# A stream of Fourier, mixing and token steps on one core: product sums over two steps, other buffers, later weight tasks

## The chip, the cores and the metric

One core of a Trainium2 chip runs the whole program. The metric is the device time of one execution in microseconds. Times of one kernel vary by some tenths of a per cent between runs, so a median of runs is given. The profile is of one further execution.

## What is computed

```
X = rfft(x, axis=1)                         # x: 8 x 3008 x 256
Yr = Xr @ w_r - Xi @ w_i + b_r ; Yi = Xr @ w_i + Xi @ w_r + b_i
Y = soft_threshold(Yr, 0.01) + 1j * soft_threshold(Yi, 0.01)
a = irfft(Y, n=3008, axis=1)                # 8 x 3008 x 256
u = a + (relu(a^T @ w_tok1) @ w_tok2)^T     # w_tok1: 3008 x 256, w_tok2: 256 x 3008
out = u + relu(u @ w_ch1) @ w_ch2           # w_ch1: 256 x 1536, w_ch2: 1536 x 256
```

The weights of the last two lines come as 64-bit numbers and are narrowed to 32 bits on the chip. Products that need full precision are made of three, with each operand split into a high and a low part (`hi * hi + hi * lo + lo * hi`).

## The kernel before

The length 3008 is 47 x 64, and the transform is done in two stages. The batch is worked in five *units*: batch entries 0 and 1 alone, then three pairs (`UNITS`, line 23). Three parts of the program follow each other.

**The start** (`begin`) takes unit 0 through the transform, makes the transformed token weights, and runs the 47-point stage of unit 1 beside it, one *row* at a time. A unit has 13 rows (`NG`). `row47` does one row n and prepares the following: it loads the row n + 4 (SP queue), makes the sum and the difference of the two halves of row n + 2 (`sum_diff`, lines 253 to 259: sum on GpSimd, L257, difference on VectorE, L258, into a tile `sd`), splits row n + 1 into high and low parts (ScalarE casts, VectorE subtracts into `xl`), and multiplies row n (`stage1`, products named `p`, six of 512 columns for a unit of two entries), evicts it on ScalarE and stores it to `a_d`. From its iteration 7 on (`FIRST47`) the start does a row in each of its remaining 15 iterations. The mixing weights are kept as sums in tiles of the tags `gh` and `gl` until `split_mix` splits them.

**The stream** (`stream`) takes units 1 to 4 through the 64-point stage, the mixing and the way back, in 84 steps: 12 for unit 1 and 24 for each pair, a step being one pair of frequencies and one batch entry. An iteration n works on several steps at once:

```
mix_a(n - 2)    6 products into p1 (bank "pm"); VectorE adds the bias: p2 = p1 + bias (L561)
forward2(n)     4 products px; ScalarE and VectorE split the result into xth and xtl, GpSimd a third of xtl (L550)
inverse(n - 4)  6 products pi for each pair of steps, evicted by ScalarE and stored to b_d
tokens(n - 4 or n - 5)  12 products gp, accumulated over the unit
mix_b(n - 2)    12 products added to p2 (named p); soft threshold z on ScalarE and VectorE; yh on ScalarE, yl on GpSimd
row47()         at some n: a row of the next unit (at47 spreads the 13 rows over the steps of the unit before)
tasks           loads, widenings and stores of the channel and token weights, 90 pieces at an even pace
```

`MIX` is the 2 and `LAG` the 4. The two p2 banks are used in turn; `p1`, `px`, `pi`, `pm` and the row's `p` share four PSUM banks that go round (`bank`, tag `w`). A widening (`narrow`, L167 to L177) is two ScalarE and six VectorE operations. `PACE` spreads the 90 pieces from n = 2 on, 1.25 x 90 / 84 = 1.34 in each n. The order in each engine's queue is laid out by a scheduler when the program is built.

**The channel stage** (`channel7`) takes the 24064 tokens in 24 chunks of 1024 (the last 512). In a chunk, 42 slots t each issue three products of the first channel product (`sx`, `sw`, `fq`) and three of the second (`s`), in an order written out by hand and kept. Between them stand the token products for the next chunk: a *group* of 4 or 5 times 94 tokens has two parts (`make_parts`), each six products with the weights `wt` and eight or ten small ones with `b`, into one bank `pu` that ScalarE then copies to `uf`. A chunk has two or three groups, and a table `makes` says at which slot each part stands: the last group at 22 and 26, the one before at 13 and 17, the first of three at 4 and 8. When the second part is issued, the loads of the next group are issued on SP (`load_wt2`, `load_b2`). Where that group is the first of a unit, `fetch_g` loads `gh` and `gl` of the unit after it first (L421).

Of the kernel before, what the change touches and what calls it, by code (L numbers as in the profile page):

```python
# [11 lines left out]
F32 = mybir.dt.float32  # L12
# [29 lines left out]
AT = (0, 3, 4, 1, 5, 6, 2)  # L42
MIX, LAG = 2, 4
FIRST47 = 7
PACE = 1.25

# [85 lines left out]
def tile_kernel(ctx: ExitStack, tc: tile.TileContext, io):  # L132
# [9 lines left out]
    dram = ctx.enter_context(tc.tile_pool(name="dram", bufs=1, space=bass.MemoryType.DRAM))  # L142
    ps = ctx.enter_context(tc.tile_pool(name="ps", bufs=4, space=bass.MemoryType.PSUM))
    sums, pairs2 = ExitStack(), ExitStack()
# [82 lines left out]
    def ev(shape, name):  # L227
        return wk.tile(shape, F32, tag="ev", name=name, bufs=2)

    def t4(shape, name):  # L230
        return wk.tile(shape, F32, tag="t4", name=name, bufs=2)
# [20 lines left out]

    def sum_diff(x, g, w, eng, pool):
        if eng is None:
            return x
        sd = wk.tile([120, 2, w], F32, tag="xf", name="sd", bufs=2) if pool is None else wk.tile([120, 2, w], F32, tag=("xtl", "xf", "et")[g % 3], name="sd", bufs=3 if g % 3 == 0 else 2)
        eng.tensor_tensor(out=sd[:, 0], in0=x[:, 0], in1=x[:, 1], op=ALU.add)  # L257
        V.tensor_tensor(out=sd[:, 1], in0=x[:, 0], in1=x[:, 1], op=ALU.subtract)  # L258
        return sd
# [6 lines left out]
    def stage1(sd, dst, g, w, pool):  # L266
        n = GS if g < NG - 1 else N2 - GS * (NG - 1)
        a = ev([120, 2, w], "a") if pool is None else pool.tile([120, 2, w], F32, name="a", bufs=3)
        each = 512 // w
        for i0 in range(0, 2, each):  # L270
            pt = bank("p1")
            for i in range(i0, i0 + each):
                o = (i - i0) * w
                if pool is None:
                    mm3(pt[:, o:o + w], f1r[:, 0, i], f1r[:, 1, i], sd[0][:, i], sd[1][:, i], True, True)
                else:
                    PE.matmul(pt[:120, o:o + w], lhsT=f1[:, i], rhs=sd[:, 0], start=True, stop=False)
                    PE.matmul(pt[:120, o:o + w], lhsT=f1[:, 2 * i], rhs=sd[:, 1], start=False, stop=True)
            S.copy(out=a[:, i0:i0 + each].rearrange("p i w -> p (i w)"), in_=pt[:120])
        rows = dst.rearrange("(i n) k w -> (n k) i w", i=2)  # L280
        PUT.dma_start(out=rows[g * 120:g * 120 + n * KH, :, :w], in_=a[:n * KH])
# [142 lines left out]
    def parts(u):  # L424
# [40 lines left out]
        def forward(kp, b, a2):  # L465
            pt = bank("px")
            for t in range(2):
                for ab in range(2):
                    o = (2 * t + ab) * 128
                    PE.matmul(pt[:, o:o + 128], lhsT=a2[:, ab, b, t * 128:(t + 1) * 128], rhs=f2cols(2 * kp + ab), start=True, stop=True)  # L470
            xf = wk.tile([128, 3, 4, 64], F32, tag="xth", name="xf", bufs=3)
            S.copy(out=xf[:, 1:3], in_=pt.rearrange("p (q i m) -> p i q m", i=2, m=64))
            V.tensor_tensor(out=xf[:, 0], in0=xf[:, 1], in1=xf[:, 2], op=ALU.add)
            return xf
# [20 lines left out]
        def inverse(kp, e, y, pool=None):  # L495
            bt = ev([128, 2, w], "bt") if pool is None else pool.tile([128, 2, w], F32, name="bt", bufs=3)
            each = 512 // w
            for i0 in range(0, 2, each):
                pt = bank("pi")
                for i in range(i0, i0 + each):  # L500
                    o = (i - i0) * w
                    if plain:
                        PE.matmul(pt[:, o:o + w], lhsT=e[:, i], rhs=y[:, i], start=True, stop=True)
                    else:
                        mm3(pt[:, o:o + w], e[:, 0, i], e[:, 1, i], rows(y, 0, i), rows(y, 1, i), True, True)
                S.copy(out=bt[:, i0:i0 + each].rearrange("p i w -> p (i w)"), in_=pt)
            PUT.dma_start(out=bdv[kp, :, :, :, :w], in_=bt)
# [27 lines left out]
        def forward2(b, a2, kp):  # L535
            pt = bank("px")
            for t in range(2):
                for ab in range(2):
                    o = (2 * t + ab) * 128
                    PE.matmul(pt[:, o:o + 128], lhsT=a2[:, ab, b, t * 128:(t + 1) * 128], rhs=f2cols(2 * kp + ab), start=True, stop=True)  # L540
            xh = wk.tile([128, 3, 4, 64], F32R, name="xth", bufs=3)
            xl = wk.tile([128, 3, 4, 64], F32R, name="xtl", bufs=3)
            xs = wk.tile([128, 4, 64], F32, name="xs", bufs=2)
# [14 lines left out]
        def mix_a(xt, p2):  # L558
            p1 = bank("pm")[:, :C]
            part(p1, xt, 0, 0, True)  # L560
            V.tensor_tensor(out=p2.rearrange("p (i c) -> p i c", i=2), in0=p1.rearrange("p (o c) -> p o c", o=1).to_broadcast([128, 2, C]), in1=bias, op=ALU.add)  # L561
# [20 lines left out]
    def beside(u):  # L582
# [7 lines left out]
        def add(g):  # L590
            if g < NG:
                sums_[g] = sum_diff(xs.pop(g), g, p.w, G, None)

# [26 lines left out]
    def stream(tasks):  # L620
# [3 lines left out]
        for i, (u, g) in enumerate(rows47):  # L624
            if u == 1 or i < done47["n"]:
                continue
            prev = first[u - 1]
            room = first[u] - 3 - prev
            at47.setdefault(prev + g * room // NG, []).append(i)
        a2s, xts, ys, ets = {}, {}, {}, {}  # L630
# [26 lines left out]
        need(1)  # L657
        pace, left, finished = PACE * len(tasks) / len(steps), 0.0, 0
        for n in range(len(steps) + LAG + 2):
# [19 lines left out]
            for m in (n - LAG, n - LAG - 1):  # L679
                if 0 <= m < len(steps):  # L680
                    u, kp, b = steps[m]
                    if b == len(UNITS[u]) - 1 and (n - m == LAG) == (b == 0):
                        parts_of(u).tokens(kp, wts_[kp], ys.pop((u, kp)))
                        if kp == KP - 1:
                            parts_of(u).close()
            ready(n - 2)
            if 0 <= c < len(steps):
                u, kp, b = steps[c]
# [5 lines left out]
            for _ in at47.get(n, ()):  # L694
                row47()
            if n > 1:
                left += pace
# [12 lines left out]
    def weights_tasks(kind, p):  # L710
# [11 lines left out]
        def widen():  # L722
            t = got["t"] = wc["task"].tile([128, 2, 512], F32, tag="wide", name="wide")
            narrow(got.pop("raw"), t[:, 0], t[:, 1])
# [29 lines left out]
    def tokens_tasks(i, jt):  # L754
# [9 lines left out]
        def widen():  # L764
            t = wc["task"].tile([128, 2, 512], F32, tag="wide", name="wide")
            wf = narrow(got.pop("raw")[:, :n], t[:, 0, :n], t[:, 1, :n])
            o = wc["task"].tile([128, 2, 512], F32R, tag="so", name="so")
            split(o[:, 0, :n], o[:, 1, :n], wf, S, V)
            got["o"] = o
# [8 lines left out]
    def begin():  # L778
# [7 lines left out]
        with tc.tile_pool(name="early", bufs=1) as early:  # L786
# [25 lines left out]
            for n in range(NW + KP):  # L812
# [26 lines left out]
                if n == FIRST47 - 1:  # L839
# [5 lines left out]
                    sides[u].divide(g)  # L845
                if n >= FIRST47:
                    row47()
# [237 lines left out]
    def channel7():  # L1085
# [14 lines left out]
        wc["pu"] = ps3.tile([128, 512], F32, name="pu")  # L1100
        wc["fq"] = bank("fq")
        for g in needs[0]:
# [25 lines left out]
        for n in range(len(chunks)):  # L1128
# [3 lines left out]
            for i, g in enumerate(mine):  # L1132
                m = make_parts(g, True)
                first = 22 - 9 * (len(mine) - 1 - i)
                makes[first], makes[first + 4] = (m, g), (m, g)
            for g in range(2):
# [91 lines left out]
```

## Time and profile before

| | us |
|---|---|
| median of 3 runs | 2361.85 (2357.34 to 2363.17) |
| profiled execution | 2356.0 |
| its span | 2354.2 |
| TensorE busy in the span | 2267.6 (96%) |
| VectorE busy | 2024.0 (86%) |
| ScalarE busy | 1667.2 (71%) |
| GpSimd busy | 279.6 (12%), all in the start and the stream |
| mean granted TensorE clock | 0.988 |

The start ends at about 156 us of the span, the stream at about 713 us; the rest is the channel stage. A product's busy time includes its way through the array, and the next one starts before it ends, so that a busy share of 96% is not 96% of the pace that is possible: the pace is read from the starts of products.

### The profile page before, as it was taken

The numbers are of one execution on the slowest core, as the hardware profiler recorded it, in microseconds if no ns is written. First come the engines' busy times: TensorE is split into PE (matmuls) and PEld (weight loads), VectorE is DVE, ScalarE is ACT, GpSimd is POOL, SyncE is SP. The second block draws the span as 40 slices with busy tenths as digits, with TensorE's granted clock in tenths as the row PEclk, the third lists the DMA queues.
The fourth block names the chain that finished last, engine by engine and source line by source line (L and its number), as shares of the span: only waits on it lengthen the run. The fifth ranks groups of instructions, "written<-read, shape, count | busy, mean of one in ns | idle before, by whom it ended". The sixth has DMA issues, their size and how long they took to land.

```text
span 2354.2 us, 34225 instructions
## 1 busy us (share of the span) xinstructions
PE 2267.6 (96%) x11844; PEld 1939.2 (82%) x11844; DVE 2024.0 (86%) x3307; ACT 1667.2 (71%) x3156; POOL 279.6 (12%) x236
## 2 busy tenths in 40 slices
PE   8997999989999999999999999999999999999999
PEld 7777878779897878888888887888888888888887
DVE  7757998998744889979999997989998998998999
ACT  6566666677655777767777776777777777777776
POOL 0135554444330000000000000000000000000000
PEclk9998999999999999999999999999999999999999
DMA  8789887776537444454444445444545445445435
GB/s 212 229 260 310 266 273 228 248 242 233 197 125 247 142 142 145 142 163 136 138 131 150 148 139 159 138 136 138 150 149 151 148 130 149 125 141 160 144 106 161
DMA packets 205610, 407.88 MB, mean 173 GB/s; under 512 B 17093, under 2 KB 108829, under 8 KB 205437
## 3 DMA queue, kind: packets, MB, share of 16 engines
q1 hardware_dynamic: 175369, 351.16, 49.6%
q10 hardware_dynamic: 30068, 54.53, 6.9%
q8 instruction: 94, 1.54, 0.3%
q14 instruction: 79, 0.65, 0.1%
HBM read 303.00 MB, written 102.63 MB: 172 GB/s over the span
## 4 chain that ended last, share of the span: by engine, by line
PE 73%; DVE 8%; DMA 5%; ACT 1%; issue 1%; POOL 0%; SPq 0%; POOLq 0%; ACTq 0%; DVEq 0%
PE s L945 27%; PE sx L945 16%; PE sw L945 8%; PE pu L945 5%; PE pu L911 5%; PE fq L945 4%; PE p L556 3%; DMA b<-b_d 2%; DMA wt<-wt_d 1%; PE px L540 1%; PE pm L556 1%; DVE sd L258 1%; PE gp L204 1%; PE gp L205 1%; DVE p L561 1%
## 5 line engine op out<-in xcount | busy, mean ns | idle before, releaser
L945 PE MATMUL s<-rh,a2s 128*128 128x512 f32 (+1 forms) x2016 | 775.4, 387 | 0.8 <-ACT rh L153 0.8
L945 PE MATMUL sx<-ub,a 128*128 128x512 f32 (+1 forms) x1728 | 489.4, 392 | 1.8 <-DVE c L1001 1.1
L945 PEld LDWEIGHTS s<-rh,a2s 128*128 128x128 f32 x2016 | 379.3, 189 | 77.1 <-ACT rh L153 1.4
L156 DVE TENSOR_TENSOR rl<-c,rh 128x512 fp32r<-128x512 f32 (+1 forms) x576 | 380.1, 677 | 57.7 <-ACT rh L153 49.3
L945 PE MATMUL s<-rl,a2s 128*128 128x512 f32 (+1 forms) x1008 | 390.6, 388 | 0.7 <-DVE rl L156 0.2
L153 ACT CAST rh<-c 128x512 fp32r<-128x512 f32 (+1 forms) x576 | 338.7, 612 | 57.7 <-DVE rl L1045 21.8
L945 PEld LDWEIGHTS sx<-ub,a 128*128 128x128 f32 x1728 | 319.1, 190 | 64.3 <-DVE c L1001 2.4
L945 PE MATMUL sw<-ub,a 128*128 128x512 f32 (+1 forms) x864 | 240.3, 387 | 1.4 <-DVE ub L156 1.1
L945 PEld LDWEIGHTS s<-rl,a2s 128*128 128x128 f32 x1008 | 190.0, 188 | 40.4 <-DVE rl L156 2.9
L153 ACT CAST rh<-r 128x512 fp32r<-128x512 f32 (+1 forms) x288 | 174.2, 613 | 50.0 <-PE s L945 37.4
L1070 DVE TENSOR_TENSOR uf<-s,uf 128x512 f32<-128x512 f32 (+1 forms) x288 | 194.3, 675 | 13.1 <-PE s L945 12.5
L156 DVE TENSOR_TENSOR rl<-r,rh 128x512 fp32r<-128x512 f32 (+1 forms) x288 | 189.3, 675 | 1.3
L945 PEld LDWEIGHTS sw<-ub,a 128*128 128x128 f32 x864 | 160.5, 188 | 35.0 <-DVE ub L156 1.4
L917 ACT COPY uf<-pu 128x470 f32<-128x470 f32 (+31 forms) x158 | 61.1, 415 | 147.5 <-PE pu L911 136.4
L911 PEld LDWEIGHTS pu<-g,b 96*128 96x128 f32 x1024 | 132.8, 196 | 9.1 <-DMA b<-b_d 6.1
L156 POOL TENSOR_TENSOR yl<-z,yh 128x512 fp32r<-128x512 f32 x84 | 121.5, 1447 | 153.2 <-ACT yh L153 148.2
L911 PE MATMUL pu<-g,b 96*128 96x94 f32 x1024 | 133.4, 277 | 2.2 <-DMA b<-b_d 2.1
L945 PE MATMUL pu<-wt,gh 128*128 128x470 f32 (+1 forms) x424 | 118.4, 361 | 11.7 <-DMA wt<-wt_d 10.7
L1045 DVE SCALAR_TENSOR_TENSOR rl<-c,rh 128x512 fp32r<-128x512 f32 (+1 forms) x144 | 97.6, 678 | 29.7 <-ACT rh L1044 29.5
L945 PE MATMUL fq<-ub,a 128*128 128x512 f32 (+1 forms) x432 | 122.2, 392 | 0.0
L982 ACT COPY c<-sw 128x512 f32<-128x512 f32 (+1 forms) x144 | 83.3, 578 | 45.1 <-PE sw L945 43.3
L1005 ACT ACTIVATE r<-sx 128x512 f32<-128x512 f32 (+1 forms) x144 | 85.2, 592 | 39.6 <-PE sx L945 36.1
(158 smaller groups left out, 4726.9 us busy)
## 6 DMA issues: line engine op xcount, KB each, us to landing
a2s<-a_d SPq DMA_DIRECT2D x336, 384.0 KB, 3.0
wt<-wt_d SPq DMA_DIRECT2D x32, 940.0 KB, 6.3
out<-uf SPq DMA_DIRECT2D x78, 256.0 KB, 3.4
x<-in_x SPq DMA_DIRECT2D x39, 480.0 KB, 5.6
a<-a_d SPq DMA_DIRECT2D x36, 512.0 KB, 4.6
b_d<-bt ACTq DMA_DIRECT2D x36, 512.0 KB, 4.9
wt<-wt_d SPq DMA_DIRECT2D x24, 752.0 KB, 5.9
a_d<-a ACTq DMA_DIRECT2D x36, 480.0 KB, 5.0
```

The source lines that it names most:

```text
L153: S.copy(out=hi, in_=src)
L156: lo_eng.tensor_tensor(out=lo, in0=src, in1=hi.bitcast(F32), op=ALU.subtract)
L204: PE.matmul(out, lhsT=wh, rhs=xl, start=False, stop=False, skip_group_check=more)
L205: PE.matmul(out, lhsT=wl, rhs=xh, start=False, stop=stop, skip_group_check=more)
L556: PE.matmul(out, lhsT=xt[x][:, j, t], rhs=w_[:, wsel, t], start=start and t + i == 0, stop=t == 1 and i == 2, skip_group_check=True)
L911: m = PE.matmul(pt[:, s * TOKS:(s + 1) * TOKS], lhsT=b2[:, s, cs], rhs=g2[:, 0 if s0 + s == 0 else 1], start=False, stop=s == k - 1, skip_ ...
L917: S.copy(out=ufs[m][:, ct, lo - at:hi - at], in_=pt[:, lo - c0:hi - c0])
L945: m = PE.matmul(out, lhsT=w, rhs=x, start=start and n == 0, stop=n == 2, skip_group_check=True)
L982: S.copy(out=block(1, k), in_=w)
L1005: S.activation(out=block(3, k), in_=x, func=AF.Relu)
L1045: V.scalar_tensor_tensor(out=lo, in0=src, scalar=0.0, in1=hi.bitcast(F32), op0=ALU.max, op1=ALU.subtract)
L1070: V.tensor_tensor(out=o, in0=outs[r], in1=o, op=ALU.add)
```

## The change

- `mix_b` works one step later than `mix_a` (c is lowered by one between them), and `LAG` becomes 5.
- p1 gets a bank of its own (tag `pm`), and three banks are shared instead of four. In the channel stage `fq` lies in that bank.
- The weight tasks run from n = 6 at a pace that ends them at n = 76.
- GpSimd makes the sum and the difference of a row for units 3 and 4. `sd` lies in the tag `gh`, and the widened weights lie in the tag `gl` with two buffers.
- `xth` and `xtl` get four buffers, the evictions of the stream three (`ev4`).
- The start makes the 13 rows of unit 1 only, and the stream's rows come at n = 2 or later.
- Token products: the last group stands at slots 24 and 27, the one before at 13 and 16, the first of three at 2 and 5.

The diff, without unchanged lines:

```diff
@@ -40,9 +40,9 @@
-MIX, LAG = 2, 4
+MIX, LAG = 2, 5
-PACE = 1.25
+TASK0, TASK1 = 6, 76
@@ -140,7 +140,7 @@
-    ps = ctx.enter_context(tc.tile_pool(name="ps", bufs=4, space=bass.MemoryType.PSUM))
+    ps = ctx.enter_context(tc.tile_pool(name="ps", bufs=3, space=bass.MemoryType.PSUM))
@@ -227,6 +227,11 @@
+    def evs(shape, name):
+        if "ys" not in wc:
+            return ev(shape, name)
+        return wc["ys"].tile(shape, F32, tag="ev4", name=name, bufs=3)
+
@@ -250,12 +255,12 @@
-    def sum_diff(x, g, w, eng, pool):
+    def sum_diff(x, g, w, eng, pool, sub=V):
-        sd = wk.tile([120, 2, w], F32, tag="xf", name="sd", bufs=2) if pool is None else wk.tile([120, 2, w], F32, tag=("xtl", "xf", "et")[g % 3], name="sd", bufs=3 if g % 3 == 0 else 2)
+        sd = const.tile([120, 2, w], F32, tag="gh", name="sd", bufs=2) if pool is None else wk.tile([120, 2, w], F32, tag=("xtl", "et")[g % 2], name="sd", bufs=(4, 2)[g % 2])
-        V.tensor_tensor(out=sd[:, 1], in0=x[:, 0], in1=x[:, 1], op=ALU.subtract)
+        sub.tensor_tensor(out=sd[:, 1], in0=x[:, 0], in1=x[:, 1], op=ALU.subtract)
@@ -265,7 +270,7 @@
-        a = ev([120, 2, w], "a") if pool is None else pool.tile([120, 2, w], F32, name="a", bufs=3)
+        a = evs([120, 2, w], "a") if pool is None else pool.tile([120, 2, w], F32, name="a", bufs=3)
@@ -468,7 +473,7 @@
-            xf = wk.tile([128, 3, 4, 64], F32, tag="xth", name="xf", bufs=3)
+            xf = wk.tile([128, 3, 4, 64], F32, tag="xth", name="xf", bufs=4)
@@ -493,7 +498,7 @@
-            bt = ev([128, 2, w], "bt") if pool is None else pool.tile([128, 2, w], F32, name="bt", bufs=3)
+            bt = evs([128, 2, w], "bt") if pool is None else pool.tile([128, 2, w], F32, name="bt", bufs=3)
@@ -538,8 +543,8 @@
-            xh = wk.tile([128, 3, 4, 64], F32R, name="xth", bufs=3)
-            xl = wk.tile([128, 3, 4, 64], F32R, name="xtl", bufs=3)
+            xh = wk.tile([128, 3, 4, 64], F32R, name="xth", bufs=4)
+            xl = wk.tile([128, 3, 4, 64], F32R, name="xtl", bufs=4)
@@ -556,7 +561,7 @@
-            p1 = bank("pm")[:, :C]
+            p1 = ps.tile([128, 512], F32, tag="pm", name="pm", bufs=1)[:, :C]
@@ -589,7 +594,7 @@
-                sums_[g] = sum_diff(xs.pop(g), g, p.w, G, None)
+                sums_[g] = sum_diff(xs.pop(g), g, p.w, G, None, G if u > 2 else V)
@@ -626,7 +631,7 @@
-            at47.setdefault(prev + g * room // NG, []).append(i)
+            at47.setdefault(max(2, prev + g * room // NG), []).append(i)
@@ -655,7 +660,7 @@
-        pace, left, finished = PACE * len(tasks) / len(steps), 0.0, 0
+        pace, left = len(tasks) / (TASK1 - TASK0), 0.0
@@ -684,6 +689,7 @@
+            c = n - MIX - 1
@@ -693,7 +699,7 @@
-            if n > 1:
+            if n >= TASK0:
@@ -720,7 +726,7 @@
-            t = got["t"] = wc["task"].tile([128, 2, 512], F32, tag="wide", name="wide")
+            t = got["t"] = const.tile([128, 2, 512], F32, tag="gl", name="wide", bufs=2)
@@ -762,7 +768,7 @@
-            t = wc["task"].tile([128, 2, 512], F32, tag="wide", name="wide")
+            t = const.tile([128, 2, 512], F32, tag="gl", name="wide", bufs=2)
@@ -843,7 +849,7 @@
-                if n >= FIRST47:
+                if n >= FIRST47 and done47["n"] < NG:
@@ -1098,7 +1104,7 @@
-        wc["fq"] = bank("fq")
+        wc["fq"] = ps.tile([128, 512], F32, tag="pm", name="fq", bufs=1)
@@ -1131,8 +1137,8 @@
-                first = 22 - 9 * (len(mine) - 1 - i)
-                makes[first], makes[first + 4] = (m, g), (m, g)
+                first = 24 - 11 * (len(mine) - 1 - i)
+                makes[first], makes[first + 3] = (m, g), (m, g)
```

## Rows read from the trace of the kernel before

**Rows 1.** Busy time by stretch (PE, PEld, DVE, ACT, POOL; clock; DMA share; GB/s).
```profile
0.00:155.70 155.70, 140.08 (x812) 118.25 (x813) 103.23 (x200) 87.35 (x156) 19.41 (x21) 1.00 0.81 229
155.70:255.70 100.00, 80.85 (x508) 72.32 (x508) 79.83 (x101) 66.34 (x130) 56.55 (x42) 0.90 0.93 293
255.70:569.30 313.60, 289.24 (x1863) 256.00 (x1862) 277.11 (x426) 221.07 (x445) 147.30 (x120) 1.00 0.78 248
569.30:636.70 67.40, 64.30 (x422) 58.08 (x422) 57.53 (x103) 45.24 (x97) 28.33 (x26) 0.97 0.65 217
636.70:713.40 76.70, 76.35 (x500) 69.34 (x499) 31.06 (x53) 40.29 (x82) 28.00 (x28) 1.00 0.45 139
```

**Rows 2.** Timeline of TensorE, start and duration, near the stream's end.
```profile
673.21 1.06 PE L540 MATMUL px<-f,a 128*128 128x128 f32 x8
...
680.61 0.39 PE L203 MATMUL gp<-yh,wt 128*128 128x512 f32 x1
680.83 0.39 PE L204 MATMUL gp<-yl,wt 128*128 128x512 f32 x1
...
683.44 0.83 PE L540 MATMUL px<-f,a 128*128 128x128 f32 x6
```

**Rows 3.** VectorE's groups, steps 12 to 59 (busy us, mean ns; idle before).
```profile
L561 DVE TENSOR_TENSOR p<-pm,bias 128x512 f32<-128x512 f32 x48 | 33.3, 693 | 27.5 <-PE pm L556 27.5
L156 DVE TENSOR_TENSOR xl<-sd,xh 120x1024 fp32r<-120x1024 f32 x25 | 31.1, 1246 | 2.7 <-ACT xh L153 2.6
L258 DVE TENSOR_TENSOR sd<-x 120x512 f32<-120x512 f32 x23 | 29.1, 1264 | 0.4
```

**Rows 4.** Waits of TensorE, steps 12 to 59: us in total, times, longest.
```profile
PE px L540 <- DVE p L561: 13.3, 12, 2.5
PE p L556 <- DVE p L561: 2.4, 2, 1.8
```

**Rows 5.** Timeline of ScalarE and TensorE, step 4 of the stream.
```profile
192.79 0.40 ACT L153 CAST et<-ef 128x256 fp32r<-128x256 f32 x1 [6.38 <-DMA ef<-in_e]
194.77 1.22 PE L203 MATMUL p<-xh,f1r 120*128 120x512 f32 x2 [8.41 <-ACT xh L153]
```

**Rows 6.** Timeline of TensorE and SP around the three waits for token weights.
```profile
830.49 0.67 PE L945 MATMUL pu<-wt,gh 128*128 128x470 f32 x2 [2.65 <-DMA wt<-wt_d]
...
1030.55 0.38 SPq L421 DMA_DIRECT2D gl<-g_d  x1
1030.98 0.53 SPq L882 DMA_DIRECT2D wt<-wt_d  x1
...
1037.13 0.39 PE L945 MATMUL s<-rh,a2s 128*128 128x512 f32 x1
1040.64 1.12 PE L945 MATMUL pu<-wt,gh 128*128 128x470 f32 x2 [3.12 <-DMA wt<-wt_d]
...
1454.59 0.67 PE L945 MATMUL pu<-wt,gh 128*128 128x470 f32 x2 [3.59 <-DMA wt<-wt_d]
```

**Rows 7.** Busy time by stretch behind the second wait, and in an undisturbed stretch.
```profile
1035.00:1060.00 25.00, 21.89 (x89) 18.28 (x88) 17.50 (x29) 12.46 (x24) 0.00 (x0) 0.80 0.59 175
1525.00:1550.00 25.00, 25.00 (x123) 21.18 (x122) 22.86 (x38) 19.77 (x38) 0.00 (x0) 1.00 0.52 152
```

**Rows 8.** Groups of GpSimd, steps 12 to 59.
```profile
L156 POOL TENSOR_TENSOR yl<-z,yh 128x512 fp32r<-128x512 f32 x47 | 70.0, 1490 | 60.9 <-ACT yh L153 56.0 <-DMA b_d<-bt 2.7 <-PE p L205 1.8
L257 POOL TENSOR_TENSOR sd<-x 120x512 f32<-120x512 f32 x23 | 36.8, 1598 | 11.5 <-DVE xl L156 5.2 <-issue 3.0 <-PE px L540 1.9
```

**Rows 9.** Line 258, steps 12 to 59: duration in ns, min/median/max.
```profile
L258 DVE TENSOR_TENSOR sd<-x x23: 678/1186/1784, 266.5 to 520.2; 120x512 f32<-120x512 f32 x23
```

**Rows 10.** Waits of GpSimd in the start.
```profile
POOL sd L257 <- DVE xl L156: 42.5, 11, 7.7
```

**Rows 11.** Timeline of ScalarE, and the chain, at a token group's two parts.
```profile
1007.16 0.47 ACT L917 COPY uf<-pu 128x376 f32<-128x376 f32 x1
...
1012.62 1.03 PE pu L945 x6
```

## The prediction

> **What bounds the kernel now.** I read the busy time by stretch first, then inside each stretch the view that says who waits. The stretches are cut where the first `px` product of the 1st, 13th, 61st and 73rd step of the stream begins, and at the first `pu` product of the channel stage. The reader is to see that TensorE is far from idle everywhere, and yet only one of the four stretches of the stream runs at its own pace [rows 1].
>
> That pace is seen near the end of the stream, where nothing else runs: from one `px` to the second next one, a pair of steps, 10.23 us pass, so a step of TensorE costs 5.1 us, and a 512-column product 0.22 to 0.23 us [rows 2]. A 47-point row adds six such products, 1.4 us.
>
> Steps 12 to 59: 48 steps cost 245 us of products and 24 rows 33 us, together 279; they take 313.6 [rows 1]. So 35 us are lost here. VectorE is busy for 277.1 of them, nearly what TensorE needs, and the two wait for each other in turn: VectorE stands 27.5 us before the sum `p` of L561 until the `pm` products have come [rows 3], and TensorE stands 13.3 us before `px` and 2.4 us before the `p` products until that sum is made [rows 4]. The cause is in the order: `mix_a` makes p1, VectorE must put it into p2, and in the same step `mix_b` adds to p2, with only `px` and the inverse or token products (0.8 + 1.4 or 2.8 us) as cover. The bank of `pm` also goes round among the four that `px` takes, so a late sum stops `px` too.
>
> Steps 0 to 11: about 62 us of step products and 11 rows of 1.4 us, 77 in all, take 100 us. The DMA engines are 93% busy there, and the granted clock is 0.90 [rows 1]. One wait stands out: ScalarE waits 6.4 us for a load `ef`, and TensorE 8.4 us for what is queued behind it on ScalarE [rows 5].
>
> Steps 60 to 83 and the tail: 67.4 us for twelve steps (61 at pace), then full pace, with VectorE at 31.1 of 76.7 us because the weight tasks are over [rows 1].
>
> Channel stage: TensorE is full but for three places. There `pu` waits 2.65, 3.12 and 3.59 us for `wt` [rows 6]. The load is issued when the group before is done, but the next unit's `gh` and `gl` go out ahead of it on SP: `wt` leaves at 1030.98 and its products start at 1040.64, while TensorE had run out of other work by 1037.4. The granted clock falls behind such a wait: this stretch has 0.80 and 89 products, where an undisturbed one with the same load of token products has 123 [rows 7]. The 34 missing, at 25 us / 123 each, are 6.9 us; for three places I estimate 20 us, waits included.
>
> **The change, part by part.** 0.3%, 7 us, is about what a measurement of this kernel can tell from no change.
>
> *Two steps for a product sum, a bank for p1.* `mix_b` of a step comes one step after its `mix_a`; nothing is added. The sum L561 then has a whole step (5 us) of cover, and `pm`, alone in its bank, is wanted again a step later. Both waits of [rows 4] should go, and the 27.5 us of [rows 3] become harmless, since VectorE is late for nothing. What is late next: `px` needs the bank that the subtraction `xtl` of an earlier step empties, now among three banks instead of four, so a VectorE queue that runs behind still shows there.
>
> *GpSimd takes both sums.* For units 3 and 4 VectorE loses 23 to 24 subtractions, 29.1 us [rows 3]; GpSimd gains as many operations of about 1.6 us, and from 147.3 of 313.6 us goes to some 185 [rows 1, 8]. Beside GpSimd VectorE slows: the same subtraction takes 0.68 us at best, and 1.26 on average with the addition running beside it [rows 3, 9]. If each moved sum stretches one VectorE operation by that 0.58 us, 13 us come back.
>
> *Weight tasks.* Their 90 pieces now run from step 6 to 76 (1.29 a step) instead of 2 to 69 (1.34), 4% less in each step: about 4 us of VectorE in steps 12 to 59. VectorE's account there is then 277 - 29 + 13 - 4 = 257 us against TensorE's 279: TensorE is the bound. The stretch cannot go below 279; of the 35 us lost I take two thirds, **-22** (bounds -35 and 0), because an in-order VectorE at 90% will still be late now and then.
>
> *Steps 60 to 83.* Tasks last seven steps longer, under TensorE's pace (57.5 us of VectorE in 67.4 before), and the waits on L561 go: **-1** (-6 to +4).
>
> *Steps 0 to 11.* The start makes 13 rows instead of 15, so 13 and not 11 fall here, and none before step 2, where the formula puts five at once. The two rows add 2.8 us of products and 2 x 1.25 us each of subtraction and split; these sums of unit 2 stay on VectorE. Tasks leave steps 2 to 5: five pieces, with three loads of about 0.5 MB, against two more row loads of 0.48 MB and two more row stores. DMA and VectorE thus come out about even. SP: the row loads of step 2 stand ahead of the weight and `a` loads of the next steps. I take **0**; if the one long wait goes, -8; if there is one more like it with a slow clock behind, +13.
>
> *Start.* Two rows less, -2.8 us of products; three shared banks instead of four, since p1's own bank is idle there: a wait for a ScalarE copy, of the length of the 0.47 us of [rows 11], in some of the 22 iterations. The buffers for `sd` are shared with the mixing sums until these are split, so one is left; GpSimd already waits 42.5 us there for VectorE to give `sd` back [rows 10], and nothing on TensorE followed it. **+2** (-3 to +8).
>
> *Buffers* (`xth`, `xtl`, evictions, `wide`) cost nothing in time. `gh` and `gl` of the first two units can now be fetched only when the tasks end; the DMA engines are 45% busy from 636.7 on [rows 1], which hides 1 MB. Without that cover it is 3 us, at the 293 GB/s of steps 0 to 11.
>
> *One more step of lag*: the drain grows by at most a step, **+1** (0 to +5).
>
> *Token products.* A group's parts stand three slots apart instead of four, groups eight slots instead of five behind the last part. A slot is six products, 1.36 us. The `wt` load gets 3 x 1.36 = 4.1 us more: products due at 1037.4 would be due at 1041.5, after the 1040.64 at which the data were there [rows 6]. Three slots between parts still leave room: the copy of the first part ends at 1007.63 and the second part starts at 1012.62, 5 us later, of which 1.4 go [rows 11]. **-17** of the 20 (bounds -22 and 0), since the margin is under 1 us.
>
> **Sum**: -22 - 1 + 0 + 2 + 1 - 17 = -37. The profiled execution took 2356.0 us; the median of the runs is 2361.85, 5.85 above it. 2356.0 - 37 = 2319.0, and on the level of the median **2325**.
>
> **Rivals.**
> - *VectorE stays the bound.* The waits move to `px <- xtl`, since GpSimd's longer hold slows the weight tasks more than the 13 us. For it: VectorE is 88% busy and in order. Only the channel part and the small terms are left: -17 + 2 + 1 = -14, **2348**. The Trainium skill, GPSIMD Engine Reference, section Key points, has a rule that speaks for this rival and against the change: GpSimd shares its SBUF interfaces with VectorE, and VectorE instructions with two SBUF inputs contend with it. The trace agrees as far as it goes, 0.68 to 1.78 us for one and the same subtraction [rows 9]; by the rule alone, every such instruction of the weight tasks would pay, and the time would be this rival's.
> - *`wt` is late still.* The margin of 0.9 us is thin, and the load shares the DMA engines with `gh` and `gl`. Stream alone: -20, **2342**.
> - *GpSimd becomes the stop, and it is slower.* In steps 12 to 59 two sums of 1.6 to 1.7 us stand back to back ahead of `xtl` and `yl`, for which TensorE waits. If 24 rows each hold TensorE for the 1.7 us added, that is +41, and the 13 us of slower VectorE come on top: -37 + 41 + 13 = +17, about **2379**. It decides from 1.5 us per row (37 / 24). Against it: GpSimd is idle for half of the stretch [rows 1, 8].
> - *No change.* The order in each queue is laid out by a scheduler and not by the source; the split could dissolve there, or step 2 could give back what the rest wins: about **2360**.
>
> **How the numbers follow.** Forecast 0.55, VectorE 0.20, `wt` 0.08, GpSimd 0.12, no change 0.05. Range 2296 to 2354: down three quarters of the way to the lower bounds together (-35 - 6 - 8 - 3 + 0 - 22 = -74, 2288), up past the two weaker gains; GpSimd and no change, 0.17, are left out. Faster 0.81, same 0.06, slower 0.13: the first three cases less a little, no change, and GpSimd.
>
> **What would show it.** Right: no wait of `px` or `p` on L561 in steps 12 to 59, that stretch near 290 us, L258 of units 3 and 4 on GpSimd, no `pu` wait above 1 us on `wt`, a clock of 1.00 through the channel stage. Wrong: TensorE waiting for `yl` or `xtl` of GpSimd more than 2 us in total per two rows, a stall with a low clock near step 2, or `wt` still waited for.

## The result, and the profile after

The changed kernel took 2323.24 us (median of 4 runs, 2320.01 to 2328.48), the kernel before 2362.51 (4 runs). The ratio is 0.9838, with a 95% interval of 0.9811 to 0.9865: faster by 32 to 45 us. The profiled execution took 2325.07 us, its span is 2323.3, 30.9 below the span before.

Busy time by stretch of the changed kernel (length, then PE, PEld, DVE, ACT, POOL with their instructions, clock, DMA share, GB/s), cut at the same products as [rows 1], with the channel stage as last row:

```profile
0.00:156.70 156.70, 141.83 (x815) 118.74 (x816) 102.36 (x201) 87.14 (x157) 20.65 (x21) 0.99 0.79 223
156.70:250.30 93.60, 75.92 (x477) 68.68 (x476) 69.84 (x83) 61.85 (x120) 62.09 (x45) 0.89 0.94 290
250.30:558.60 308.30, 289.20 (x1869) 260.67 (x1868) 261.85 (x392) 220.53 (x441) 184.77 (x145) 0.98 0.78 249
558.60:625.40 66.80, 64.10 (x429) 58.13 (x428) 65.97 (x126) 48.71 (x105) 27.01 (x24) 1.00 0.76 255
625.40:704.50 79.10, 78.93 (x518) 71.93 (x517) 34.19 (x57) 42.74 (x86) 30.14 (x30) 1.00 0.47 152
704.50:2323.30 1618.80, 1605.96 (x7747) 1359.51 (x7746) 1477.60 (x2426) 1207.30 (x2248) 0.00 (x0) 1.00 0.48 148
```

Line numbers of the changed kernel are up to six higher: L566 is the sum of p1 that was L561, L554 the subtraction `xtl`, L262 and L263 are sum and difference.

By these two profiles 22 of the 31 us lie in the channel stage, 1640.8 to 1618.8 us, and 6.5 in steps 0 to 11. Steps 12 to 59, where most was expected, gave 5 us, though VectorE is busy for 15 us less there. (How the gain divides between the last two depends on the cut, since the order of the products around it changed: cut two steps later, their 11.7 us divide into 2.3 and 9.4.) The waits of TensorE in steps 12 to 59 (us in total, times, longest):

```profile
PE px L545 <- DVE xtl L554: 9.1, 6, 2.9
PE pm L561 <- DVE p L566: 2.8, 4, 1.4
PE pi L203 <- ACT so L153: 2.0, 2, 1.6
...
PE pi L204 <- POOL yl L156: 0.5, 1, 0.5
```

The waits of [rows 4] are gone: `px` no longer waits for the sum of p1, the `p` products neither, and `pm` does a little (2.8 us). In their place `px` waits 9.1 us for `xtl`, the subtraction that empties its bank. All waits of TensorE in the stretch together fell from 24.1 to 18.9 us. But behind waits at 268.8, 292.1 and 497.1 us the granted clock went to 0.50 (1.2 GHz in place of 2.4), for 10.2 us in all, and in the kernel before it stayed at 1.00 throughout these steps. At half pace that is a loss of about 5 us, an estimate, and as much as the shorter waits gave.

What holds `xtl` up is seen in VectorE's groups in steps 12 to 59 (count | busy us, mean ns | idle before). First two groups of the kernel before, then, of the changed kernel, two that read PSUM and the same two again:

```profile
L172 DVE TENSOR_SCALAR wide<-wide 128x512 f32<-128x512 f32 (+2 forms) x18 | 16.6, 923 | 0.0
...
L174 DVE SCALAR_TENSOR_TENSOR wide<-wide 128x512 uint32<-128x512 uint32 (+2 forms) x18 | 13.4, 742 | 0.6
```

```profile
L566 DVE TENSOR_TENSOR p<-pm,bias 128x512 f32<-128x512 f32 x48 | 33.2, 693 | 5.5 <-PE pm L561 4.1
L574 DVE SCALAR_TENSOR_TENSOR z<-p,z 128x512 f32<-128x512 f32 x48 | 32.9, 686 | 13.6 <-ACT z L573 13.4
L172 DVE TENSOR_SCALAR wide<-wide 128x470 f32<-128x470 f32 (+2 forms) x18 | 21.7, 1206 | 1.3 <-ACT wide L167 1.3
L174 DVE SCALAR_TENSOR_TENSOR wide<-wide 128x470 uint32<-128x470 uint32 (+2 forms) x18 | 21.3, 1186 | 0.3
```

The weight tasks got longer, L174 from 0.74 to 1.19 us, and the six VectorE lines of a widening together from 81.2 us for 110 operations to 97.8 us for 111, while L566, which reads PSUM and SBUF, has the 693 ns of [rows 3] still. The timeline of the changed kernel shows how one of the two longest of the six waits for `xtl` comes about:

```profile
487.99 1.53 DVE L172 TENSOR_SCALAR wide<-wide 128x512 f32<-128x512 f32 x1
489.55 1.67 DVE L174 SCALAR_TENSOR_TENSOR wide<-wide 128x512 uint32<-128x512 uint32 x1
491.25 1.40 DVE L175 TENSOR_SCALAR wide<-wide 128x512 uint32<-128x512 uint32 x1
...
487.70 1.53 POOL L156 TENSOR_TENSOR yl<-z,yh 128x512 fp32r<-128x512 f32 x1
489.19 1.48 POOL L262 TENSOR_TENSOR sd<-x 120x512 f32<-120x512 f32 x1
490.62 1.74 POOL L263 TENSOR_TENSOR sd<-x 120x512 f32<-120x512 f32 x1
...
497.13 1.08 PE L545 MATMUL px<-f,a 128*128 128x128 f32 x5 [2.87 <-DVE xtl L554]
```

From 487.7 to 492.4 us GpSimd is never idle, and three VectorE operations take 4.6 us; where GpSimd is idle beside them they take 0.42, 0.69 and 0.42, 1.5 together. The lines after them are back at 0.69 us, but `px` has been waiting since 494.3. In the 12 us before each of the other five waits, too, one of the lines 172 to 174 took over 1.4 us beside a busy GpSimd.

In the channel stage the timeline of the changed kernel at the place of [rows 6] shows the group's load on SP, and what waits now:

```profile
1014.35 0.38 SPq L426 DMA_DIRECT2D gl<-g_d  x1
1014.78 0.53 SPq L888 DMA_DIRECT2D wt<-wt_d  x1
...
1026.92 0.47 PE L951 MATMUL s<-rh,a2s 128*128 128x512 f32 x1 [1.73 <-DVE r L1046]
...
1027.69 0.59 PE L951 MATMUL pu<-wt,gh 128*128 128x470 f32 x2
```

`wt` leaves at 1014.78, and its products come 12.9 us later, without a wait. At the three places TensorE still waits 1.0 to 1.7 us, twice for `a2s` and once for VectorE, and the clock does not fall there. It does fall at the start of the channel stage: `pu` waits 2.2 us for `b` at 719.1 us, and the granted clock is 0.50 from 719.4 to 733.0. In the kernel before it was 0.50 for 6.8 us at that start, and for 23.9 us behind the three waits for `wt`. The stretch that answers to the first of [rows 7], by busy time:

```profile
1010.00:1035.00 25.00, 23.27 (x114) 19.58 (x113) 21.07 (x34) 16.69 (x31) 0.00 (x0) 1.00 0.64 209
```

114 products in 25 us instead of 89, at a clock of 1.00.

### The profile page after: what moved, and what is told of

The parts are those of the page before. It is cut to its first block, busy times and chain, and to the rows that moved or that the text cites. A ratio compares the mean times of both kernels' runs of the same rounds, so it can differ in the third digit from the quotient of the medians.

```text
span 2323.3 us, 34243 instructions
## 1 busy us (share of the span) xinstructions
PE 2255.9 (97%) x11844; PEld 1937.7 (83%) x11844; DVE 2011.8 (87%) x3281; ACT 1668.3 (72%) x3156; POOL 324.7 (14%) x262
## 4 chain that ended last, share of the span: by engine, by line
PE 76%; DVE 8%; ACT 3%; issue 2%; DMA 1%; POOL 0%; SPq 0%; POOLq 0%; ACTq 0%; DVEq 0%
PE s L951 28%; PE sx L951 16%; PE sw L951 8%; PE pu L951 5%; PE pu L917 5%; PE fq L951 4%; PE p L561 2%; PE px L545 2%; PE pm L561 1%; DVE wide L174 1%; PE gp L203 1%; PE gp L205 1%; PE gp L204 1%; DVE wide L172 1%; DVE rl L156 1%
## 5 line engine op out<-in xcount | busy, mean ns | idle before, releaser
L156 POOL TENSOR_TENSOR yl<-z,yh 128x512 fp32r<-128x512 f32 x84 | 127.5, 1518 | 141.3 <-ACT yh L153 131.9
L982 ACT COPY fq<-sx 128x512 f32<-128x512 f32 (+1 forms) x144 | 81.1, 564 | 41.0 <-PE sx L951 39.0
```

What stands on the lines that cost most here:

```text
L156: lo_eng.tensor_tensor(out=lo, in0=src, in1=hi.bitcast(F32), op=ALU.subtract)
L982: S.copy(out=q, in_=x)
```

## The experiments

Lengths of the stretches in each profile, in us, from the first `px` of steps 0, 12, 60 and 72, the first `pu` product and the span:

| kernel | start | 0-11 | 12-59 | 60-71 | 72-end | channel |
|---|---|---|---|---|---|---|
| before | 155.8 | 100.1 | 313.5 | 67.3 | 76.7 | 1640.8 |
| changed | 156.7 | 93.6 | 308.3 | 66.8 | 79.2 | 1618.7 |
| spacing only | 155.7 | 101.4 | 315.0 | 67.4 | 76.7 | 1621.1 |
| difference on VectorE | 155.8 | 90.9 | 301.4 | 66.8 | 79.2 | 1627.2 |
| both on VectorE | 153.6 | 90.3 | 290.2 | 66.8 | 79.2 | 1617.9 |
| one step | 153.7 | 85.5 | 310.4 | 69.7 | 76.7 | 1619.2 |
| both on VectorE, one step | 156.2 | 90.8 | 300.5 | 69.7 | 76.7 | 1621.2 |
| before, both on VectorE | 160.1 | 99.9 | 299.8 | 67.4 | 76.7 | 1638.7 |
| unit 2 on VectorE too | 156.5 | 87.8 | 290.9 | 66.8 | 79.2 | 1622.4 |
| tasks from step 2 | 154.1 | 93.3 | 291.6 | 64.7 | 79.2 | 1625.3 |
| four banks | 155.7 | 89.4 | 293.7 | 65.8 | 79.4 | 1617.9 |
| rows spread | 154.5 | 89.0 | 289.8 | 66.8 | 79.2 | 1621.3 |
| `xtl` on VectorE | 153.9 | 87.3 | 296.9 | 64.4 | 79.2 | 1624.9 |

The channel stage differs by up to 9 us among kernels that have the same one in the source, so a single profile tells less of it than of the stream. Part of the difference is the clock: with the new slots it stood at 0.50 in that stage for between 6.8 us (one step) and 20.5 us (difference on VectorE), most of it in the first 45 us, largely behind waits for `b` and `wt`. Ratios below are to runs of the kernel before on the same chip. Every edit also lets the scheduler lay out the queues anew, so a wait can move by the order as well as by the engine that was changed.

**Token spacing alone**, on the kernel before:

```diff
-                first = 22 - 9 * (len(mine) - 1 - i)
-                makes[first], makes[first + 4] = (m, g), (m, g)
+                first = 24 - 11 * (len(mine) - 1 - i)
+                makes[first], makes[first + 3] = (m, g), (m, g)
```

> The kernel before with the new slots of the token products and nothing else. Theory: the two parts of the change add up and do not touch each other, and the channel stage gains what it gained in the changed kernel, 22.0 us (1640.8 to 1618.8): about 2340, ratio 0.990 to before, no wait for the token weights above 1 us and no low clock behind one. Rival: the loads come early enough only because the changed stream hands over earlier or leaves other buffers; then one or more of the three waits stay and the gain is under 12 us.

2342.75 us, ratio 0.9935 (0.9919 to 0.9951): a gain of 15 us (12 to 19), less than the 22 expected. In the profile the channel stage is 19.7 us shorter. The mechanism of the theory holds, its size does not: at none of the three places does TensorE wait for `wt` any more, it waits 1.5 to 2.2 us for `a2s` there, and the clock stays at 1.00 behind it. The spacing works by itself. How much is left for the rest of the change is less clear: 23 us by the difference of the two ratios, 9 us by the stretches of the two profiles.

**The difference back on VectorE**, on the changed kernel:

```diff
-                sums_[g] = sum_diff(xs.pop(g), g, p.w, G, None, G if u > 2 else V)
+                sums_[g] = sum_diff(xs.pop(g), g, p.w, G, None, V)
```

> The changed kernel with the differences of units 3 and 4 on VectorE again, the sums still on GpSimd. Theory: giving the difference to GpSimd won little, because GpSimd's longer hold slows VectorE's weight tasks (L172 from 0.92 to 1.21 us, L174 from 0.74 to 1.19) by about what the 29 us of subtractions relieve; within 8 us of the changed kernel (2323). Rival: the difference on GpSimd is what brought the stream's gain; then steps 12 to 59 go back to 313 us or more, and the kernel to about 2332 to 2345.

2319.9 us, ratio 0.984 (0.9819 to 0.9861), the changed kernel's. Steps 12 to 59 are even shorter in its profile, 301.4 us. Giving the difference to GpSimd won nothing.

**Both on VectorE**, on the changed kernel:

```diff
-                sums_[g] = sum_diff(xs.pop(g), g, p.w, G, None, G if u > 2 else V)
+                sums_[g] = sum_diff(xs.pop(g), g, p.w, V if u > 2 else G, None, V)
```

> The changed kernel with both sum and difference of units 3 and 4 on VectorE, so that GpSimd does no 47-point sums in steps 12 to 59. Theory of contention: without GpSimd beside it VectorE makes each in 0.68 us, 1.36 us a row, hardly more than the 1.26 us that the difference alone took before, and the weight tasks keep their short durations (L174 below 0.85 us); VectorE's busy time in steps 12 to 59 is 262 + 32 - 20 = about 274 us, and the kernel is 0 to 12 us above the changed one. Rival, contention is nothing: VectorE gets 47 operations more and no relief, 262 + 32 = 294 us, above TensorE's 279; the stretch takes 325 us or more and the kernel is 15 us or more above the changed one.

2301.9 us, ratio 0.9768 (0.9748 to 0.9788): faster than both kernels, by 0.7% or 16 us than the changed one going by the ratios, which neither theory nor rival had expected. Steps 12 to 59 by busy time, and VectorE's groups there:

```profile
243.90:534.10 290.20, 284.25 (x1867) 256.54 (x1868) 266.48 (x439) 220.72 (x441) 122.38 (x99) 1.00 0.81 265
```

```profile
L172 DVE TENSOR_SCALAR wide<-wide 128x470 f32<-128x470 f32 (+2 forms) x18 | 11.8, 654 | 1.2 <-ACT wide L167 1.1
...
L174 DVE SCALAR_TENSOR_TENSOR wide<-wide 128x470 uint32<-128x470 uint32 (+2 forms) x18 | 11.7, 650 | 0.1
...
L262 DVE TENSOR_TENSOR sd<-x 120x512 f32<-120x512 f32 x23 | 23.8, 1034 | 0.3
L263 DVE TENSOR_TENSOR sd<-x 120x512 f32<-120x512 f32 x23 | 16.7, 726 | 0.0
```

VectorE takes over 46 operations, 40.5 us, and its busy time rises from 261.9 to 266.5 us only. L172 falls from 1.21 to 0.65 us, L174 from 1.19 to 0.65. TensorE now waits 2.1 us for `xtl` in place of 9.1:

```profile
PE px L545 <- DVE xtl L554: 2.1, 3, 1.5
PE gp L203 <- ACT yh L153: 1.9, 3, 1.5
```

All waits of TensorE in the stretch come to 5.7 us where the changed kernel has 18.9, and the clock stays at 1.00: 13 us of waits and about 5 us of lost clock make up the 18 us between the two. The stretch lies 11 us above the 279 us that the prediction took as TensorE's need; less the waits it is 284.5, so that by this count 279 was some 5 us too low.

The traces also tell whether it is GpSimd that stretches these operations. Over all 13 of them, among operations of 512 columns, those of the widening lines 172 to 177 and VectorE's sums and differences are never long when GpSimd does nothing beside them: with one SBUF input at most 0.44 us in 713 cases, with two at most 0.71 us in 1081. With a GpSimd operation beside them they take up to 1.53 us (262 cases) and 1.80 us (570 cases), about half of them clearly longer. The sum of p1, `xtl` and `z`, which read PSUM, take at most 0.70 us in 3276 cases, with GpSimd beside them or not.

**One step again**, on the changed kernel (p1 keeps its bank):

```diff
-MIX, LAG = 2, 5
+MIX, LAG = 2, 4
-            c = n - MIX - 1
```

> The changed kernel with both halves of a product sum in one step again (lag 4), p1 still in its own bank, all else changed. Theory: the wait of the p2 products for L561 comes back, the wait of px for L561 does not, since the bank is separate; TensorE loses 5 to 12 us more in steps 12 to 71: about 2328 to 2335. Rival: VectorE bounds steps 12 to 59 whatever the order, and nothing changes (within 4 us). Second rival: the split is the whole gain of the stream, and the kernel goes to about 2340 or above.

2321.74 us, ratio 0.9857 (0.9835 to 0.9879), not to be told from the changed kernel: the first rival. The waits did come back as the theory has it, and something else was paid back. Waits of TensorE in steps 12 to 59 of this run, then in steps 60 to 71:

```profile
PE p L561 <- DVE p L566: 7.8, 11, 2.6
...
PE px L545 <- DVE xtl L554: 0.8, 1, 0.8
```

```profile
PE p L561 <- DVE p L566: 5.0, 4, 2.2
```

The wait only changes its name: 7.8 us for the sum of p1 here, 9.1 us for `xtl` there. Steps 60 to 71 take 2.9 us more, and the drain is 2.5 us shorter, which is what the further step of lag costs at the end. That steps 0 to 11 look 8 us shorter here is the cut: in this order the `px` of step 12 stands earlier, and counted to that of step 13 it is 97.9 us against 100.6.

**One step, both sums on VectorE**: the two edits together.

> The kernel with both sums of units 3 and 4 on VectorE (2301.9), with the product sum in one step again (lag 4). Theory: the split pays once VectorE is not slowed by GpSimd. With one step the p products wait for L566 again (7.8 us in steps 12 to 59 and 5.0 us in steps 60 to 71 in the earlier run with one step), and px runs behind; 3 to 12 us slower: 2305 to 2314. Rival: the split is worth nothing, as it was with the sums on GpSimd: within 3 us of 2302.

2314.95 us, ratio 0.9823 (0.981 to 0.9836), 13 us slower than with two steps; the intervals do not meet. Steps 12 to 59 take 300.5 us and not 290.2, and the `p` products wait 5.6 us for L566 again. With both sums off GpSimd the split is worth 10 us of the stretch; with them on it, no gain of it could be told from noise.

**The kernel before with both sums on VectorE**:

```diff
-                sums_[g] = sum_diff(xs.pop(g), g, p.w, G, None)
+                sums_[g] = sum_diff(xs.pop(g), g, p.w, V if u > 2 else G, None)
```

> The kernel before with both sums of units 3 and 4 on VectorE, and nothing else. Theory: contention was there before too, since sum and difference ran side by side; VectorE's busy time in steps 12 to 59 stays within 8 us of 277, GpSimd's 37 us go away, and steps 12 to 59 take 300 to 314 us: 0 to 12 us faster than before. Rival: only in the changed kernel, with split sums and its own bank, is there room for them; here VectorE gets 23 x 0.68 = 16 us more and the kernel is 5 to 20 us slower than before.

2345.14 us, ratio 0.9939 (0.9918 to 0.996). Steps 12 to 59 fall by 13.7 us to 299.8, more than twice what the whole change brought there. The theory holds, with a little more than the 12 us that it named at most: 14 us by the ratio (9 to 19).

Five smaller ones start from the changed kernel with both sums on VectorE.

**Unit 2 on VectorE too**:

```diff
-sum_diff(xs.pop(g), g, p.w, V if u > 2 else G, None, V)
+sum_diff(xs.pop(g), g, p.w, V if u > 1 else G, None, V)
```

> The kernel with the sums of units 3 and 4 on VectorE, and those of unit 2 as well, so that GpSimd makes 47-point sums only for unit 1. Theory: steps 0 to 11 lose by the same contention; they go from 90.3 to 82 to 89 us, the kernel to 2294 to 2300. Rival: these steps wait for loads (DMA engines 96% busy) and VectorE's queue at step 2, where five rows stand; 13 more operations of 0.7 us there make them longer by up to 9 us, 2302 to 2311.

2304.8 us, ratio 0.9775 (0.9763 to 0.9788). Steps 0 to 11 are 2.5 us shorter, the whole is not; whether unit 2 gains a little was not settled.

**Tasks from step 2 to 69**:

```diff
-TASK0, TASK1 = 6, 76
+TASK0, TASK1 = 2, 69
```

> The kernel with both sums of units 3 and 4 on VectorE, with the weight tasks from step 2 to 69 as before. Theory: holding the tasks back until step 6 is what shortened steps 0 to 11 by 6 us in the changed kernel; with them early these steps take 95 to 101 us instead of 90.3, steps 12 to 59 2 to 5 us more, and the kernel 2305 to 2315. Rival: those steps got shorter by the rows and the order, and the start of the tasks changes nothing (within 3 us of 2302).

2309.56 us, ratio 0.9799 (0.9786 to 0.9811), and the interval touches that of 0.9768. Steps 0 to 11 take 3.0 us more, steps 12 to 59 1.4 more, steps 60 to 71 2.1 less. That is some 2 us for the later start in the stream, in single profiles, and not shown: in three kernels with the same code for steps 0 to 11 these take 90.3, 90.9 and 93.6 us. Of the 10.3 us between the two profiles 7.4 lie in the channel stage, which was not changed.

**Four shared banks**:

```diff
-    ps = ctx.enter_context(tc.tile_pool(name="ps", bufs=3, space=bass.MemoryType.PSUM))
+    ps = ctx.enter_context(tc.tile_pool(name="ps", bufs=4, space=bass.MemoryType.PSUM))
-            p1 = ps.tile([128, 512], F32, tag="pm", name="pm", bufs=1)[:, :C]
+            p1 = bank("pm")[:, :C]
-        wc["fq"] = ps.tile([128, 512], F32, tag="pm", name="fq", bufs=1)
+        wc["fq"] = bank("fq")
```

> The kernel with both sums of units 3 and 4 on VectorE (2301.9), with p1 among four shared banks as before; the split over two steps stays. Theory: a bank of its own matters because px then never waits for the sum of p1; with the split alone px waits for L566 again, 5 to 10 us in steps 12 to 59: 2307 to 2313. Rival: the split over two steps gives the sum its cover already, and four banks that go round are as good as three and one: within 3 us of 2302.

2305.6 us, ratio 0.9795 (0.978 to 0.981). No wait for L566 came back, against the theory; `px` waits 5.0 us for `xtl` instead of 2.1, and steps 12 to 59 are 3.5 us longer. A bank of its own is worth 3 us or so at this place, at the edge of what the runs resolve.

**Rows of unit 2 spread** over steps 2 to 8:

```diff
-            at47.setdefault(max(2, prev + g * room // NG), []).append(i)
+            at47.setdefault(2 + g * 7 // NG if u == 2 else prev + g * room // NG, []).append(i)
```

> The kernel with both sums of units 3 and 4 on VectorE, with the 13 rows of unit 2 spread two to a step over steps 2 to 8 instead of five at step 2. Theory: the long third step (23 us) with its wait of 5.8 us and the lower clock behind it is the price of the five rows; steps 0 to 11 go from 90.3 to 83 to 87 us and the kernel to 2294 to 2299. Rival: the rows are late because of their loads and VectorE's total, not their places; nothing changes (within 3 us).

2305.66 us, ratio 0.9791 (0.9773 to 0.9809); steps 0 to 11 take 89.0 us, 1.3 less. The rival: the five rows at step 2 are not what makes these steps long. In the kernel with both sums on VectorE, VectorE waits 6.3 us there for the row loads, as its timeline shows:

```profile
170.70 0.69 DVE L263 TENSOR_TENSOR sd<-x 120x512 f32<-120x512 f32 x1 [6.33 <-DMA x<-in_x]
```

**The third part of `xtl` on VectorE**:

```diff
-            G.tensor_tensor(out=xl[:, 0], in0=xs, in1=xh[:, 0].bitcast(F32), op=ALU.subtract)
+            V.tensor_tensor(out=xl[:, 0], in0=xs, in1=xh[:, 0].bitcast(F32), op=ALU.subtract)
```

> The kernel with both sums of units 3 and 4 on VectorE, with the third part of xtl (L555, 0.9 us on GpSimd, 84 times) on VectorE too. Theory: by now VectorE has 266 us of work in steps 12 to 59 against TensorE's 279; 48 x 0.42 = 20 us more, less some 10 us of shorter weight tasks, bring it level with TensorE, and the stretch gets 0 to 8 us longer: 2302 to 2312. Rival: contention is so strong that taking any work off GpSimd pays; 3 to 10 us faster.

2305.33 us, ratio 0.9791 (0.9777 to 0.9804); steps 12 to 59 take 296.9 us, 6.7 more, with VectorE busy for 279.8 of them. Here VectorE is the fuller queue, and taking more off GpSimd no longer pays.

## Why the prediction was right, and where it was not

The forecast was 2325 and the result 2323.24, in the range and on the side foreseen. The terms, against the spans of the two profiles (the medians moved by 39 us, the spans by 31):

| term | predicted | measured |
|---|---|---|
| steps 12 to 59 | -22 | -5.2 |
| steps 60 to 83 (measured: 60 to 71) | -1 | -0.5 |
| steps 0 to 11 | 0 | -6.5 |
| start | +2 | +0.9 |
| drain, one more step of lag (measured: steps 72 to the end) | +1 | +2.5 |
| channel stage | -17 | -22.1 |
| sum | -37 | -30.9 |

That forecast and result lie 2 us apart is in part luck. The largest term missed by 17 us; steps 0 to 11, put at nothing, and the channel stage gave 11.6 us more than forecast in its place. The 6 us by which the sum still falls short are made up by the medians: that of the kernel before lies 6.5 us above its profiled execution, that of the changed kernel 2 us below. In the later sets of runs the kernel before took 2354.8 to 2356.6 us, not 2362.5.

*Channel stage: right.* The mechanism was shown by the experiment with the spacing alone. The estimate of 20 us from the missing products of [rows 7] was better than the 17 taken, going by the profiles (22.1 and 19.7); by the ratio of the spacing alone, 15 us, it was not.

*Steps 12 to 59: right on which waits go, wrong on what comes next.* The waits of [rows 4] went, as predicted, and `px <- xtl` took their place, as named. The step that failed is the sentence that TensorE is the bound because VectorE's account is 257 us, and that two thirds of the 35 us would be won. The account itself was near (261.9 measured), and so were the 13 us allowed for stretching (16.6 on the six lines of a widening). But the stretching does not lie evenly: in the timeline shown, three operations of a widening stand in a row while GpSimd works through `yl` and both sums, and 3 us of lateness in one place cost TensorE a wait, and behind it a slower clock, that an average does not show. The first rival, VectorE still the bound because GpSimd slows the weight tasks, is what happened in this stretch. That GpSimd causes it is shown by both sums on VectorE, 46 operations more for VectorE and 18 us less for the stretch, and by the count of operations with and without GpSimd beside them.

*The GpSimd rival, TensorE waiting for GpSimd itself, did not happen*: its products waited 0.5 us for `yl` in all in steps 12 to 59. GpSimd is busy 184.8 of 308.3 us, the 185 predicted. It does its harm through VectorE.

*The rule weighed in the prediction is borne out.* The Trainium skill, GPSIMD Engine Reference, section Key points, names VectorE instructions with two SBUF inputs and those in a 2-port perf mode as the ones that contend with GpSimd. The trace agrees on two inputs: L174 goes from 0.65 us on average without the sums on GpSimd to 1.67 beside them, and L566, with one of its two inputs in PSUM, stays at 0.69. L175, with one SBUF input, goes from 0.42 (its median over the changed kernel) to 1.40; whether it runs in such a mode no run here shows.

*Steps 0 to 11* gave 6.5 us that were counted as nothing (2.3 with the later cut). The wait of 8.4 us of [rows 5] went, which the prediction priced at -8. The stall with a low clock near step 2, which it priced at +13 and named as a sign of being wrong, came as well: a product of a row waits there for VectorE's split, and the clock is 0.50 from 173.2 to 180.1 us.

```profile
PE p L204 <- DVE xl L156: 5.4, 1, 5.4
```

What the later start of the tasks gave was not settled. Of the signs of being right, two did not come: steps 12 to 59 took 308.3 us and not about 290, and the clock was not 1.00 through the channel stage, as told above.

*What stays open*: what decides the waits and the low clock at the start of the channel stage, by which equal kernels differ there, and how the changed kernel's gain divides between spacing and stream, where ratios and profiles disagree.

The best kernel of the study is the changed one with both sums of units 3 and 4 on VectorE: 2301.9 us, 2.3% below the kernel before.

## What to carry to other kernels

Before giving a full VectorE's work to an idle GpSimd, look at what VectorE does at that time: if it is SBUF work, the stretching can cost more than the work that left, as 46 moved operations were worth 4.6 us of busy time and cost 18 us. Fixing the wait that ends last can show only after the next one is gone too: the split gave nothing that could be seen until the contention went, and then 10 us. For a load that is late by a little, moving its user by a few slots was enough (moving the load was not tried), and it saved the low clock behind the wait as well.

## What the runs showed of the hardware that was not expected

Beside GpSimd a VectorE operation on SBUF of 512 columns takes up to 1.1 us longer, with one SBUF input (0.42 to 1.53 us) as with two (0.68 to 1.80), and one that reads PSUM takes no longer at all. In proportion the single input is stretched most: in the changed kernel L175 took 0.42 us as its median and up to 1.48 us, 3.5 times, the longest where GpSimd was busy beside it; the subtraction of two SBUF inputs [rows 9] 2.6 times, from 0.68 to 1.78. L175 in the whole changed kernel (duration in ns, min/median/max):

```profile
L175 DVE TENSOR_SCALAR wide<-wide x39: 337/424/1484, 28.1 to 617.2; 120x512 uint32<-120x512 uint32 x13, 128x512 uint32<-128x512 uint32 x12, 128x470 uint32<-128x470 uint32 x8, 128x376 uint32<-128x376 uint32 x6
```
